# Mamba2 scan and SiLU block on one core: four PSUM banks shared by the scan and a correction sum, and another step plan

## The chip, the core and the metric

The kernel runs on one NeuronCore of a Trainium2 chip. The core has TensorE (PE, matmuls, with its weight loads shown as PEld), VectorE (DVE), ScalarE (ACT), GpSimd (POOL) and SyncE (SP, which here issues nearly all DMAs). Matmuls write to PSUM, which this program divides into eight banks of 128 x 512 fp32; everything else lives in SBUF. Each engine takes its instructions in the order in which the program issues them and waits on semaphores for the others. The metric is the time of one execution on the device in microseconds. Before the change it is 402.47 us, the median of two runs (402.38 and 402.56).

## The reference

Inputs: x (4 batches, 8 heads, 768 positions, 32), decays a (4, 8, 768), B and C (4, 8, 768, 16), w_in (256 x 2048) and w_out (2048 x 256), all fp32. The first half is a state-space scan in chunks; the second is a dense layer, SiLU, and a dense layer over 3072 tokens of 256 values:

```python
for c in range(nc):
    cum = np.cumsum(la, axis=-1)                       # la = log(clip(a, 1e-6, 1))
    L = np.exp(cum[:, :, :, None] - cum[:, :, None, :]) * causal
    M = np.einsum('bhin,bhjn->bhij', Cc, Bc) * L
    y[:, :, sl] = M @ xc + (Cc @ state) * np.exp(cum)[..., None]
    state = exp(sum la) * state + sum_j decay_from_j * B_j x_j
x = y.transpose(0, 2, 1, 3).reshape(3072, 256)
h = x @ w_in
g = h / (1 + np.exp(-h))
return g @ w_out
```

(The state's lines are shortened.)

## The kernel before, in words

**Tiling.** The 3072 tokens are twelve units of 256 (three a batch), in six pairs of 512 tokens, P = 0 to 5. A unit is four chunks of 64 positions: 2 halves k of 128 partitions, each with 2 chunks c. For each unit the scan does, with the letters that the step plan uses:

- T, P: transposes B and C (`f_T`, VectorE, with the scaled copies ce on ScalarE), and makes running products of the decays (`f_P`, VectorE).
- 0, 1, 2: clips the decays (`f_E0`) and makes the matrix E of all decay products with two VectorE scans (`f_E1`).
- B, C: scales B by the last column of E (BT, GpSimd) and C by the running products (cw; GpSimd except in units 1 and 2).
- G: C B' for each head (`f_G`, small matmuls, L407). M: multiplies E by it in place (`f_M`, VectorE, L413).
- D: B'x of each chunk (`f_D0`, L392). S: carries the state over the chunks (VectorE, L427), s: splits it into two masked copies (ScalarE, L434).
- Y: the output, from the state (L450) and from M (L460), and its copy to SBUF (`f_X`, xf, L471).
- h, l, d: splits xf into xh, xl and xd for the dense layers (ScalarE, GpSimd, VectorE).

**The dense layers.** Pair 0 uses plain fp32 matmuls (`f_s1`, `f_s2`), with tiles m0 to m7 of the second layer. From pair 1 on every product is made of three fp32r matmuls: a value v is split into a high part h and a low part l, and d = h - 4096 l; the product is h h' + l l' plus a correction by d d'. A step s of 80 handles one of 16 slices f of 128 hidden columns of a pair (f = s mod 16). Its first layer takes 6 matmuls: two d d' (`s1_d`, L527), a scaling of their result in PSUM by ScalarE (L529), and four on top (`s1_h`, L535). Then ScalarE makes g by SiLU (L543) and gh (L545), GpSimd gl (L549), VectorE gd (L553). The second layer runs three steps later (`s2`, LAG = 3) with 6 matmuls: two d d' (L564) and four of h and l (L567, L568), each kind summed in banks of its own over 16 steps. At a pair's end `f_out` copies both out, `f_sub` subtracts, `f_store` transposes and stores.

**The order of work.** It is written out by hand: nothing is scheduled by a planner. A list for pair 0 (`steps` and the texts with m) puts scan work for units 2 and 3 between the matmuls. Then `step(s)` issues the first layer of slice s, the second of slice s - 3, gd of s - 1 and the scan work of the next pair's units a (from f = 0) and b (from f = 6) by PLAN:

```python
PLAN = ("TP", "012BC", "GM", "gm", "DSs", "Y", "y", "hld")
```

So in step f = 7 unit a's h, l, d stand ahead of unit b's 0, 1, 2, B, C. The letters g, m and y are the second halves of G, M and Y. Loads of a unit two further on are issued behind y.

**Buffers.** PSUM: one pair of banks named gy, used in turn by both halves of G, by D and by both halves of Y; two single banks for the first layer (hp); four for the second layer's sums (two for h and l, two for d d'). A tile with one buffer can be written anew only once everything that reads it has finished. In SBUF, E, BT, ce, cw and sm have one buffer each, the loads of a unit two, x three; seven large buffers (quad) hold raw weights and later xh, xl and xd.

The weights come as raw words, are turned into fp32 (w_size on ScalarE, w_bits on VectorE and GpSimd) and split into wh, wl, wd: 0 to 9 in the prologue, 10 to 15 in pair 1.

Of the kernel before, what the change touches and what calls it, by code (L numbers as in the profile page):

```python
# [31 lines left out]
def kernel(  # L32
# [36 lines left out]
    loads = ctx.enter_context(tc.tile_pool(name="loads", bufs=2))  # L69
    quad = ctx.enter_context(tc.tile_pool(name="quad", bufs=7))  # L70
# [5 lines left out]
    ps_a = ctx.enter_context(tc.tile_pool(name="ps_a", bufs=4, space=bass.MemoryType.PSUM))  # L76
# [3 lines left out]
    NB = 66  # L80
# [8 lines left out]
    def bank2():  # L89
        return ps_s.tile([128, 2, 512], FP32, name="gy")  # L90
# [24 lines left out]
    def load_n(u, i, q):  # L115
        b, t0 = at(u)
        if i == 0:
            t = bn[u] = loads.tile([128, 2, H, N], FP32, name="bn")
        else:
            t = tbc[u] = loads.tile([128, 2, 2, 8, N], FP32, name="tbc")[:, 0]  # L120
        for k in range(2):
            q.dma_start(out=t[:, k], in_=(B, C)[i][b, :, t0 + 128 * k:t0 + 128 * k + 128].rearrange("h p n -> p h n"))

    def load_t(u, i, q):
        b, t0 = at(u)
        if u not in tbc:
            tbc[u] = loads.tile([128, 2, 2, 8, N], FP32, name="tbc")
        for g in range(4):
            q.dma_start(out=tbc[u][32 * g:32 * g + 32, i],
                        in_=(B, C)[i][b, 2 * g:2 * g + 2, t0:t0 + UT].rearrange("e (t r) n -> t e r n", r=8))  # L130

    def load_x(u, q):
        b, t0 = at(u)
        xt[u] = loads.tile([128, 2, H, D], FP32, name="xt", bufs=3)
        for k in range(2):
            q.dma_start(out=xt[u][:, k], in_=x[b, :, t0 + 128 * k:t0 + 128 * k + 128].rearrange("h p d -> p h d"))
# [17 lines left out]
    RAW = 7  # L154
# [59 lines left out]
    pz = const.tile([128, 8, Q + 1], FP32, name="pz")  # L214
    one = const.tile([128, 8, Q + 1], FP32, name="one")
    pfx01 = const.tile([128, 8, Q + 1], FP32, name="pfx01")
# [68 lines left out]
    E, M, BT, BH, CT, CE, CW, PFX, ST, SM, GY, XF, BX = ({} for _ in range(13))  # L285

    def f_P01():
        nc.vector.tensor_scalar(out=pz[:, :, 1:], in0=pa01.rearrange("p (c t) -> p c t", c=8), scalar1=1.0,
                                scalar2=1e-6, op0=ALU.min, op1=ALU.max)
        nc.vector.tensor_tensor_scan(out=pfx01.rearrange("p c t -> p (c t)"), data0=pz.rearrange("p c t -> p (c t)"),  # L290
                                     data1=one.rearrange("p c t -> p (c t)"), initial=0.0,
                                     op0=ALU.mult, op1=ALU.add)
        for u in range(2):
            PFX[u] = pfx01[:, 4 * u:4 * u + 4]

    def f_P0(u):
        nc.vector.tensor_scalar(out=pz[:, 0:4, 1:], in0=pa.pop(u).rearrange("p (c t) -> p c t", t=Q),
                                scalar1=1.0, scalar2=1e-6, op0=ALU.min, op1=ALU.max)

    def f_P1(u):  # L300
        PFX[u] = sc2.tile([128, 4, Q + 1], FP32, name="pfx")
        nc.vector.tensor_tensor_scan(out=PFX[u].rearrange("p c t -> p (c t)"),
                                     data0=pz[:, 0:4].rearrange("p c t -> p (c t)"),
                                     data1=one[:, 0:4].rearrange("p c t -> p (c t)"), initial=0.0,
# [73 lines left out]
    def f_D0(u, early=False):  # L378
# [3 lines left out]
        n = 3 if last else 4  # L382
        if early:
            d = [acc("bx")[:, 0:128] for c in range(2)]
        else:
            t = bank2()
            d = [t[:, c, 0:128] for c in range(2)]
        d = [o.rearrange("p (k x) -> p k x", k=2) for o in d]
        for t in range(n):
# [8 lines left out]
    def f_G(u, i):  # L398

        bh, ce = BH[u], CE[u]  # L400
        GY[u] = bank2()
        for c in range(2):
            for k in range(2):
                ts = slice(128 * k + 64 * c, 128 * k + 64 * c + 64)
                for q in range(2):
                    g = 2 * i + q
                    nc.tensor.matmul(out=GY[u][64 * c:64 * c + 64, q, 128 * k:128 * k + 128],  # L407
# [3 lines left out]
    def f_M(u, i):  # L411
        m = E[u].rearrange("p k (i q e) t -> p k i q (e t)", q=2, e=2)[:, :, i]
        nc.vector.tensor_tensor(out=m, in0=GY.pop(u)[:, :, 0:UT].rearrange("p q (k x) -> p k q x", k=2), in1=m, op=ALU.mult)  # L413
# [23 lines left out]
    def f_Y(u, e):  # L437


        sp, cw, m, xc = SM[u], CW[u], E[u], xt[u]  # L440
        y = GY[u] = bank2()
        opened = set()
        for k in range(2):
            for w in range(2):
                t = 2 * k + (w ^ e)
                if t == 0 and u % UPB == 0:
                    continue
                for q in range(2):
                    g = 2 * w + q
                    nc.tensor.matmul(out=y[64 * q:64 * q + 64, w, 64 * k:64 * k + 64],  # L450
                                     lhsT=sp[32 * g:32 * g + 32, t], rhs=cw[32 * g:32 * g + 32, Q * t:Q * t + Q],
                                     start=(w, q) not in opened, stop=False,
                                     tile_position=(32 * g, 64 * q), skip_group_check=True)
                    opened.add((w, q))
        for k in range(2):
            for w in range(2):
                c = w ^ e
                for q in range(4):
                    h = 4 * w + q
                    nc.tensor.matmul(out=y[32 * q:32 * q + 32, w, 64 * k:64 * k + 64],  # L460
                                     lhsT=xc[64 * c:64 * c + 64, k, h], rhs=m[64 * c:64 * c + 64, k, h],
                                     start=False, stop=True, tile_position=(64 * c, 32 * q), skip_group_check=True)

    def f_X(u, e):

        if e == 0:
            XF[u] = block("xf")
        y = GY.pop(u)
        o = two(XF[u]).rearrange("p w (k c t) -> p w k c t", k=2, c=2)
        for w in range(2):  # L470
            nc.scalar.activation(o[:, w, :, w ^ e], y[:, w, 0:128].rearrange("p (k t) -> p k t", k=2), AF.Copy)  # L471
# [83 lines left out]

    def s2(s):
        P, f = 1 + s // NF, s % NF
        if f == 0:
            OA[P] = [[acc("oa") for m in range(2)] for i in range(2)]
        n, r = 8 + f // 2, f % 2  # L560
        gh, gl, gd = GH.pop(s), GL.pop(s), GD.pop(s)
        for m in range(2):
            ms = slice(128 * m, 128 * m + 128)
            nc.tensor.matmul(out=OA[P][1][m], lhsT=two(WD[n])[:, r, ms], rhs=gd, start=(f == 0), stop=(f == NF - 1))  # L564
        for m in range(2):
            ms = slice(128 * m, 128 * m + 128)
            nc.tensor.matmul(out=OA[P][0][m], lhsT=two(WH[n])[:, r, ms], rhs=gh, start=(f == 0), stop=False)  # L567
            nc.tensor.matmul(out=OA[P][0][m], lhsT=two(WL[n])[:, r, ms], rhs=gl, start=False, stop=(f == NF - 1))  # L568
# [8 lines left out]
    def f_out(P):  # L577

        for m in range(2):
            t, o = block("od"), block("o")  # L580
            nc.scalar.activation(t, OA[P][1][m], AF.Copy)  # L581
            nc.vector.tensor_scalar(out=o, in0=OA[P][0][m], scalar1=UP, scalar2=None, op0=ALU.mult)
            OUT.append((P, m, o, t))
# [27 lines left out]
    f_G(0, 0)  # L611
# [4 lines left out]
    f_D0(0, True)  # L616
    f_P01()
# [4 lines left out]
    f_G(0, 1)  # L622
# [6 lines left out]
    f_Y(0, 0)  # L629
    f_X(0, 0)  # L630
    f_Y(0, 1)
    f_Ek(1, 0)
    f_Ab(1, 1)
    f_X(0, 1)
# [12 lines left out]
    f_G(1, 0)  # L647
    f_D0(1, True)
    f_M(1, 0)
    f_G(1, 1)  # L650
    f_S(1)
    f_SM(1)
    w_size(3)
    f_M(1, 1)
# [3 lines left out]
    f_Y(1, 0)  # L658
    f_X(1, 0)
    f_Y(1, 1)  # L660
    f_X(1, 1)
# [4 lines left out]
    def stage(u, what):  # L666
        for c in what:
# [20 lines left out]
            elif c in "Gg":  # L688
                f_G(u, "Gg".index(c))
            elif c in "Mm":  # L690
                f_M(u, "Mm".index(c))
            elif c == "D":
                f_D0(u)
            elif c == "S":
# [3 lines left out]
            elif c in "Yy":  # L698
                f_Y(u, "Yy".index(c))
                f_X(u, "Yy".index(c))  # L700
# [7 lines left out]
    def todo(text):  # L708

        for step in text.split():  # L710
            if ":" in step:
# [7 lines left out]
             (1, 4, "2:P0"), (0, 5, "2:12BC s9 3:L"), (1, 5, "2:GM b9 s10"), (0, 6, "2:gm"), (1, 6, "2:DSs b10 s11"),  # L719
             (0, 7, "2:Y b11 s12 3:T"), (1, 7, "2:y b12 s13 3:P0 h0"))  # L720
# [3 lines left out]
    for text in ("m0 3:12BC 2:h h1 l0 d0 2:l b13 s14", "m1 3:GM 2:d 4:L h2 l1 d1 b14 s15", "m2 3:gm h3 l2 d2 b15",  # L724
                 "m3 3:DSs h4 l3 d3", "m4 3:Y h5 l4 d4 h6", "m5 3:y l5 d5 5:L h7", "m6 3:hld l6 d6 h8", "m7 l7 d7 l8 d8 h9 o0 o1 l9 d9"):
# [5 lines left out]
    PLAN = ("TP", "012BC", "GM", "gm", "DSs", "Y", "y", "hld")  # L731
    WAITING = []

    def step(s):

        last = NF * (NP - 1)
        t = s - LAG
        ends = t >= 0 and t % NF == NF - 1
        if s < last:
            if s == 0:  # L740
                s1_d(0)
            if ends:
                s2(t)
            s1_h(s)
            if (s + 1) % NF:
                s1_d(s + 1)
            if ends:
                f_out(1 + t // NF)
            s1_g(s)
            s1_gl(s)  # L750
        if t >= 0 and (s >= last or not ends):
            s2(t)
        if s >= 1 and s - 1 < last:
            s1_gd(s - 1)
        if s >= last and ends:
            f_out(1 + t // NF)
            f_sub(nc.vector)
            f_store()
# [57 lines left out]
```

## Time and profile before

| | |
|---|---|
| median of the runs | 402.47 us |
| execution that was profiled | 407.98 us (span of the trace 406.2) |
| TensorE busy | 361.5 us (89%) |
| VectorE, ScalarE, GpSimd busy | 236.2, 214.1, 195.2 us |
| DMA | 26.37 MB, mean 65 GB/s |
| first fp32r step (s = 0) starts | 107.6 us |
| pair P = 1, then 2, 3, 4 | 61.6, then 58.7, 60.3, 58.8 us |
| last pair, without scan work, to the end | 59.2 us |
| SyncE's longest waits | for the output transposes, 214.1 us |

Times in the profile count from the first instruction. A row of a timeline or a chain gives start, duration, engine, line, operation and tiles (out<-in), then how often it is merged; in brackets stands how long the engine was idle before it and what ended that wait. Matmuls are pipelined, so a matmul's own duration (0.39) is longer than the distance to the next one (0.23); costs are read from starts. A busy share over the whole span mixes the prologue, the pairs with a scan and the last pair, so stretches are looked at one by one.

### The profile page before, as it was taken

The page shows a single profiled execution, that of the slowest core. Times are in us where ns is not written, and L with a number is a line of the kernel's source. Part 1 is how long each engine was busy: PE and PEld are TensorE (multiplying, and loading weights), DVE is VectorE, ACT ScalarE, POOL GpSimd, SP SyncE. Part 2 cuts the span into 40 slices and gives each one's busy share as a digit, 9 for nine tenths or more (in the row PEclk, how much of TensorE's full clock was granted, in tenths as well). Part 3 has the DMA queues.
Part 4 walks back from the last instruction along what each step waited for, and adds up shares of the span by engine and source line. Part 5 has one row for each costly group of instructions (what it writes and reads, how often), then busy time and mean ns, then how long its engine had stood idle before and what let it go on. Part 6 is the DMA issues. An engine that isn't in the chain of part 4 may idle for free.

```text
span 406.2 us, 7961 instructions
## 1 busy us (share of the span) xinstructions
PE 361.5 (89%) x3146; PEld 270.4 (67%) x3146; DVE 236.2 (58%) x345; ACT 214.1 (53%) x427; POOL 195.2 (48%) x168
## 2 busy tenths in 40 slices
PE   7798969989878969999979999799999799999990
PEld 3467757867656747767757767577767577768880
DVE  7377827995866574675661786541786542532223
ACT  2335726704466726665636656536656546475640
POOL 3134302476776465556353565334565445465440
PEclk9578969999999969999989999969999989999997
DMA  7887866340233150003670004750003000002003
GB/s 166 204 244 123 316 145 126 65 85 2 46 72 67 41 90 2 1 2 53 130 129 3 0 2 81 132 102 2 0 2 53 0 2 2 0 10 44 0 2 52
DMA packets 112621, 26.37 MB, mean 65 GB/s; under 512 B 102216, under 2 KB 108360, under 8 KB 112584
## 3 DMA queue, kind: packets, MB, share of 16 engines
q1 hardware_dynamic: 110504, 25.73, 30.3%
q8 instruction: 25, 0.41, 0.4%
q10 hardware_dynamic: 2080, 0.13, 0.3%
q14 instruction: 12, 0.10, 0.1%
HBM read 22.70 MB, written 3.15 MB: 64 GB/s over the span
## 4 chain that ended last, share of the span: by engine, by line
PE 50%; ACT 4%; POOL 4%; DVE 3%; issue 3%; DVEq 0%; POOLq 0%
PE hp L535 16%; PE hp L527 8%; PE oa L564 8%; PE oa L567 7%; PE oa L568 7%; POOL o L587 2%; ACT hp L529 2%; PE gy L450 1%; PE gy L407 1%; PE gy L460 1%; ACT od L581 1%; ACT g L543 1%; POOL gl L549 1%; DVE ot L596 1%; DVE E L413 1%
## 5 line engine op out<-in xcount | busy, mean ns | idle before, releaser
L549 POOL TENSOR_TENSOR gl<-g,gh 128x512 fp32r<-128x512 f32 x80 | 107.5, 1346 | 106.1 <-ACT gh L545 96.9
L553 DVE SCALAR_TENSOR_TENSOR gd<-gl,gh 128x512 fp32r<-128x512 f32 x80 | 76.0, 957 | 81.8 <-POOL gl L549 77.6
L529 ACT ACTIVATE hp<-hp 128x512 f32<-128x512 f32 x80 | 46.5, 581 | 88.4 <-PE hp L527 88.1
L535 PE MATMUL hp<-xh,wh 128*128 128x512 f32 x160 | 70.0, 437 | 6.7 <-ACT hp L529 6.4
L535 PE MATMUL hp<-xl,wl 128*128 128x512 f32 x160 | 64.8, 405 | 0.0
L567 PE MATMUL oa<-gh,wh 128*128 128x512 f32 x160 | 63.8, 399 | 0.0
L568 PE MATMUL oa<-gl,wl 128*128 128x512 f32 x160 | 63.7, 398 | 0.0
L527 PE MATMUL hp<-xd,wd 128*128 128x512 f32 x160 | 52.6, 410 | 1.2 <-ACT g L543 1.2
L545 ACT ACTIVATE gh<-g 128x512 fp32r<-128x512 f32 x80 | 50.5, 632 | 3.9
L564 PE MATMUL oa<-gd,wd 128*128 128x512 f32 x160 | 51.5, 404 | 0.0
L543 ACT ACTIVATE g<-hp 128x512 f32<-128x512 f32 x80 | 47.5, 594 | 3.0 <-PE hp L535 3.0
L535 PEld LDWEIGHTS hp<-xh,wh 128*128 128x128 f32 x160 | 30.6, 191 | 21.1 <-ACT hp L529 11.5
L191 POOL TENSOR_TENSOR w<-wu,wv 128x512 uint32<-128x512 uint32 (+1 forms) x20 | 21.5, 1082 | 43.2 <-DVE wv L186 41.8
L500 PE MATMUL hp<-xf,w 128*128 128x256 f32 x128 | 36.3, 443 | 4.7 <-DVE cw L375 3.7
L527 PEld LDWEIGHTS hp<-xd,wd 128*128 128x128 f32 x160 | 30.9, 195 | 10.2 <-ACT g L543 2.9
L564 PEld LDWEIGHTS oa<-gd,wd 128*128 128x128 f32 x160 | 31.2, 195 | 7.6
L314 DVE TENSOR_TENSOR_SCAN E<-ab,diag 128x512 f32<-128x512 f32 x24 | 32.5, 1390 | 6.3 <-PE gy L460 5.5
L500 PEld LDWEIGHTS hp<-xf,w 128*128 128x128 f32 x128 | 27.9, 224 | 11.9 <-issue 6.2
L567 PEld LDWEIGHTS oa<-gh,wh 128*128 128x128 f32 x160 | 31.0, 194 | 7.2
L568 PEld LDWEIGHTS oa<-gl,wl 128*128 128x128 f32 x160 | 30.8, 192 | 7.4
L535 PEld LDWEIGHTS hp<-xl,wl 128*128 128x128 f32 x160 | 31.0, 194 | 5.0
L407 PE MATMUL gy<-ce,bh 32*64 32x128 f32 x384 | 17.6, 297 | 15.7 <-DVE E L413 15.7
(84 smaller groups left out, 428.5 us busy)
## 6 DMA issues: line engine op xcount, KB each, us to landing
ab<-in_a_dram SPq DMA_DIRECT2D x40, 128.0 KB
raw<-in_moe_w_in_dram SPq DMA_DIRECT2D x8, 512.0 KB
raw<-in_moe_w_out_dram SPq DMA_DIRECT2D x8, 512.0 KB
xt<-in_x_dram SPq DMA_DIRECT2D x24, 128.0 KB
out_dram<-ot SPq DMA_DIRECT2D x48, 64.0 KB
bn<-in_B_dram SPq DMA_DIRECT2D x22, 64.0 KB
tbc<-in_C_dram SPq DMA_DIRECT2D x40, 32.0 KB
pa<-in_a_dram SPq DMA_DIRECT2D x10, 128.0 KB
```

Source lines behind the costliest of these rows:

```text
L314: nc.vector.tensor_tensor_scan(out=E[u].rearrange("p k h t -> p (k h t)")[:, Q * g0:Q * (g0 + n)], data0=t.rearrange("p g t -> p (g t)"), ...
L500: nc.tensor.matmul(out=hp[:, i], lhsT=two(w32[j])[:, kc, 128 * i:128 * i + 128], rhs=two(XF[u])[:, kc], start=(kc == 0), stop=(kc == KC - 1))
L527: nc.tensor.matmul(out=HP[s], lhsT=two(WD[f // 2])[:, kc, 128 * (f % 2):128 * (f % 2) + 128], rhs=XD[P][:, kc], start=(kc == 0), stop=Fals ...
L529: nc.scalar.activation(HP[s], HP[s], AF.Copy, scale=-1.0 / UP)
L535: nc.tensor.matmul(out=HP[s], lhsT=two(w[f // 2])[:, kc, 128 * (f % 2):128 * (f % 2) + 128], rhs=x_[P][:, kc], start=False, stop=(kc == KC ...
L543: nc.scalar.activation(G[s], HP.pop(s), AF.Silu, scale=UP)
L545: nc.scalar.activation(GH[s], G[s], AF.Copy, scale=DOWN)
L549: nc.gpsimd.tensor_tensor(out=GL[s], in0=G.pop(s), in1=GH[s].bitcast(FP32), op=ALU.subtract)
L553: nc.vector.scalar_tensor_tensor(out=GD[s], in0=GL[s].bitcast(FP32), scalar=-4096.0, in1=GH[s].bitcast(FP32), op0=ALU.mult, op1=ALU.add)
L564: nc.tensor.matmul(out=OA[P][1][m], lhsT=two(WD[n])[:, r, ms], rhs=gd, start=(f == 0), stop=(f == NF - 1))
L567: nc.tensor.matmul(out=OA[P][0][m], lhsT=two(WH[n])[:, r, ms], rhs=gh, start=(f == 0), stop=False)
L568: nc.tensor.matmul(out=OA[P][0][m], lhsT=two(WL[n])[:, r, ms], rhs=gl, start=False, stop=(f == NF - 1))
```

## The change

The second layer's sum of d d' gives up its own two banks and shares four banks with the scan (`bank4`). Those four serve, in turn, G and D of a unit together, its Y, and, twice a pair, a stretch of d d' sums. The scan's matmuls of a unit thus come in two bursts instead of five (G with D, Y whole). G's order of heads changes too: consecutive matmuls go to four different row groups. The d d' matmuls of a pair are put off and issued in clumps when the banks are free (`PENDING`, `s2_d`): a first segment at f = 5 to 7, a second from f = 11 to f = 2 of the next pair; after each, VectorE takes the sum to SBUF (`f_sum2`, copy and then add).

The step plan is new: h, l, d lie in steps of their own, and the weight splits 6, 7 and 9 to 15 lie in pair 1 (PARTS). The last two m pieces of pair 0 go into steps 0 and 1. `s1_d` of the next slice is issued in the same place in all steps. To make room in SBUF for 74 instead of 66 small blocks, the loads of a unit have one buffer, x two, quad six.

```diff
-    loads = ctx.enter_context(tc.tile_pool(name="loads", bufs=2))
-    quad = ctx.enter_context(tc.tile_pool(name="quad", bufs=7))
+    loads = ctx.enter_context(tc.tile_pool(name="loads", bufs=1))
+    quad = ctx.enter_context(tc.tile_pool(name="quad", bufs=6))
...
-    ps_a = ctx.enter_context(tc.tile_pool(name="ps_a", bufs=4, space=bass.MemoryType.PSUM))
+    ps_a = ctx.enter_context(tc.tile_pool(name="ps_a", bufs=2, space=bass.MemoryType.PSUM))
...
-    NB = 66
+    NB = 74
...
-    def bank2():
-        return ps_s.tile([128, 2, 512], FP32, name="gy")
+    def bank4(name="gy"):
+        return ps_s.tile([128, 4, 512], FP32, name=name, tag="gy")
...
-        xt[u] = loads.tile([128, 2, H, D], FP32, name="xt", bufs=3)
+        xt[u] = loads.tile([128, 2, H, D], FP32, name="xt", bufs=2)
...
-    RAW = 7
+    RAW = 6
...
+    def f_G(u):
+        bh, ce, dp = BH.pop(u), CE.pop(u), new_dp(u)
+        for k in range(2):
+            for c in range(2):
                 ts = slice(128 * k + 64 * c, 128 * k + 64 * c + 64)
...
+                for g in range(4):
+                    nc.tensor.matmul(out=dp[64 * c:64 * c + 64, g, 128 * k:128 * k + 128],
                                      lhsT=bh[32 * g:32 * g + 32, ts], rhs=ce[32 * g:32 * g + 32, :, ts],
                                      start=True, stop=True, tile_position=(32 * g, 64 * c), skip_group_check=True)
...
+    def f_sum2(P):
+
+        b2 = B2.pop(P)
+        if P not in SUM2:
+            SUM2[P] = [block("sum2") for m in range(2)]
+            for m in range(2):
+                nc.vector.tensor_copy(out=SUM2[P][m], in_=b2[:, m])
+        else:
+            for m in range(2):
+                nc.vector.tensor_tensor(out=SUM2[P][m], in0=b2[:, m], in1=SUM2[P][m], op=ALU.add)
...
+        f_sum2(P)
         for m in range(2):
-            t, o = block("od"), block("o")
-            nc.scalar.activation(t, OA[P][1][m], AF.Copy)
-            nc.vector.tensor_scalar(out=o, in0=OA[P][0][m], scalar1=UP, scalar2=None, op0=ALU.mult)
-            OUT.append((P, m, o, t))
+            o = block("o")
+            nc.scalar.activation(o, OA[P][m], AF.Copy, scale=UP)
+            OUT.append((P, m, o, SUM2[P][m]))
...
-    for text in ("m0 3:12BC 2:h h1 l0 d0 2:l b13 s14", "m1 3:GM 2:d 4:L h2 l1 d1 b14 s15", "m2 3:gm h3 l2 d2 b15",
-                 "m3 3:DSs h4 l3 d3", "m4 3:Y h5 l4 d4 h6", "m5 3:y l5 d5 5:L h7", "m6 3:hld l6 d6 h8", "m7 l7 d7 l8 d8 h9 o0 o1 l9 d9"):
+    for text in ("m0 3:12CB 2:h h1 l0 d0 2:l b13 s14", "m1 3:D 2:d 4:L h2 l1 d1 b14 s15", "m2 3:SsM h3 l2 d2 b15",
+                 "m3 3:Y h4 l3 d3", "m4 3:h h5 l4 d4 h8 3:l", "m5 3:d l5 d5 5:L l8 d8"):
         todo(text)
...
-    PLAN = ("TP", "012BC", "GM", "gm", "DSs", "Y", "y", "hld")
-    WAITING = []
+
+    PLAN = {0: ("aTP0",), 1: ("a12CB",), 2: ("aD",), 3: ("aSsM", "bL"), 4: ("aY",), 5: ("ah", "bTP0"), 6: ("al", "b12CB"),
+            7: ("ad",), 8: ("bD",), 9: ("bSsM", "aL"), 10: ("bY",), 11: ("bh",), 12: ("bl",), 13: ("bd",)}
+    PENDING = []
+
+    PARTS = {0: 9, 2: 10, 4: 11, 5: 6, 6: 12, 8: 7, 9: 13, 11: 14, 13: 15}
...
+        if ends and scans:
+            end()
         if s < last:
...
+        if PENDING and not (scans and (f < 5 or 8 <= f < 11)):
+            s2_d(PENDING)
+            PENDING.clear()
+        if scans and f == 7:
+            f_sum2(P)
```

In the new plan D stands for `f_G` and `f_D0` together, M for both halves, Y for the whole output and its copy, L for the loads of a unit. `scans` is true while a next pair remains to be scanned, and `ends` in the step in which a pair's last slice reaches the second layer (f = 2 of the next pair); there `end()` issues the clump of d d' and the last h and l matmuls first of all.

## The prediction

> **What bounds the kernel now.** I read the page first: shares of busy time and the slices.
>
> ```profile
> PE 361.5 (89%) x3146; PEld 270.4 (67%) x3146; DVE 236.2 (58%) x345; ACT 214.1 (53%) x427; POOL 195.2 (48%) x168
> PE   7798969989878969999979999799999799999990
> ...
> PEclk9578969999999969999989999969999989999997
> DMA  7887866340233150003670004750003000002003
> ```
>
> TensorE is nearly always busy, DMA is not after the first quarter, and the clock row has a dip once a pair (slices 15, 21, 27, 33). The second view, busy time by stretch, gives the pairs P = 2, 3, 4 and then the last pair with the tail:
>
> ```profile
> 71.20:107.60 36.40, 32.72 (x297) 26.64 (x282) 29.32 (x39) 14.56 (x32) 22.84 (x18) 1.00 0.22 42
> 107.60:169.20 61.60, 52.60 (x486) 38.32 (x486) 37.95 (x52) 36.14 (x72) 38.08 (x30) 0.94 0.29 52
> 169.20:227.90 58.70, 54.99 (x504) 41.02 (x504) 34.95 (x51) 34.04 (x68) 29.66 (x25) 0.97 0.30 55
> 227.90:288.20 60.30, 56.44 (x497) 41.89 (x497) 34.64 (x50) 34.06 (x68) 29.33 (x25) 0.94 0.30 54
> 288.20:347.00 58.80, 55.01 (x504) 40.99 (x504) 34.64 (x50) 34.08 (x68) 29.57 (x25) 0.97 0.06 10
> 347.00:406.20 59.20, 48.87 (x208) 38.76 (x208) 19.91 (x28) 29.10 (x51) 24.54 (x19) 0.96 0.11 19
> ```
>
> After the length of each stretch come PE, PEld, DVE, ACT, POOL, then the granted clock. A pair takes 58.7 to 60.3 us. The chain, in the last pair where no scan runs, shows what a step costs when only TensorE counts:
>
> ```profile
> 365.42 0.93 PE hp L535 x4
> ...
> 368.20 0.93 PE hp L535 x4
> ```
>
> The pitch is 2.78 us for twelve matmuls, 0.232 each: 16 steps are 44.5. The rest of a scanning pair, 14 to 16 us, is small matmuls and waits. The timeline of TensorE shows both:
>
> ```profile
> 199.12 0.39 PE L568 MATMUL oa<-gl,wl 128*128 128x512 f32 x1
> 199.44 0.68 PE L407 MATMUL gy<-ce,bh 32*64 32x128 f32 x16
> 200.05 0.50 PE L535 MATMUL hp<-xh,wh 128*128 128x512 f32 x1
> 200.38 0.40 PE L535 MATMUL hp<-xl,wl 128*128 128x512 f32 x1
> ...
> 205.61 0.68 PE L407 MATMUL gy<-ce,bh 32*64 32x128 f32 x16 [2.51 <-DVE E L413]
> 206.22 0.68 PE L535 MATMUL hp<-xh,wh 128*128 128x512 f32 x1
> 206.70 0.63 PE L535 MATMUL hp<-xl,wl 128*128 128x512 f32 x1
> ```
>
> From 199.12 to 200.38 is 1.26 us; two ordinary spacings (0.46) would have been there anyway, so half a G costs 0.80, of which 0.61 is the burst and 0.19 entry and exit. The same subtraction gives 0.58 for D (185.27 to 186.31) and 0.96 for half a Y (192.59 to 194.01). A unit is 2 x 0.80 + 0.58 + 2 x 0.96 = 4.1 us, two are 8.2. So 52.7 of a pair is work, and 6 to 7.6 us is lost. Most of that is at 205.61: the second half of G waits 2.51 us for VectorE, and then the matmuls run at a spacing of 0.43 instead of 0.23 (step 10 takes 4.90 us where 3.36 are due). Together 4.2 us a pair, more in the two pairs whose clock stays low for longer. VectorE's timeline tells why:
>
> ```profile
> 199.85 0.69 DVE L490 SCALAR_TENSOR_TENSOR xd<-xl,xh 128x512 fp32r<-128x512 f32 x1 [3.62 <-POOL xl L486]
> ...
> 201.41 2.34 DVE L314 TENSOR_TENSOR_SCAN E<-ab,diag 128x512 f32<-128x512 f32 x2
> 203.66 0.67 DVE L553 SCALAR_TENSOR_TENSOR gd<-gl,gh 128x512 fp32r<-128x512 f32 x1
> 204.86 0.69 DVE L413 TENSOR_TENSOR E<-gy,E 128x512 f32<-128x512 f32 x1 [0.53 <-POOL BT L347]
> ```
>
> In step 7 the xd of unit a stands ahead of unit b's scans, and waits 3.62 us for an xl issued to GpSimd in the same step. The scans come late by that, then the first M, and the second G needs the banks that this M reads.
>
> [...] the idle 2.51 us is followed by 3.4 us at a spacing near 0.43, while an idle 1.58 us (at 88.97) leaves the clock at 1.00. [...]
>
> **The change, part by part.**
>
> *Bursts.* G and D become one burst, Y one. Three entries and exits a unit go: at least 3 x 0.19 = 0.57. G now alternates over eight tile positions instead of four; its 32 matmuls lie between 0.61 (all parallel) and 1.22 (no gain); I take 0.75. With D (0.39) and one entry: 1.33. Y: 1.92 less 0.19 to 0.5, since the change between the two kinds inside it also goes once; I take 1.5. Sum 2.8 a unit (2.6 to 3.5), 1.3 less than now.
>
> *Step plan.* xh, xl, xd of unit a move to steps 5, 6, 7, its scans' neighbours to 6: the wait of xd is gone, M doesn't stand between two halves of G. That takes away the 4.2 us of every pair, if nothing replaces it. s1_d of the next pair is issued in its ordinary place in step 15 and not at the end: step 15 falls from 3.62 to 2.78, 0.8 a pair.
>
> *d d' sum.* The same 32 matmuls a pair, only clumped; cost 0 on TensorE. The sum now leaves PSUM in two pieces: two PSUM reads more on VectorE a pair, near 0.68 each (as M and the o copy, 0.683 and 0.668), in place of nothing. VectorE has the time on average (35 of 59 us), but the first piece's two reads stand between its scans and G. Step 8: the clump and steps 5 to 7 give TensorE 3.7 + 2.8 + 2.8, and G is due 2.3 later, 11.6 us after step 5 begins. VectorE starts a gd at 2.0, then come transposes, prefix scan and clip (3.1), a gd, two scans (2 x 1.43) and the reads (1.36): with gd at 0.67 to 0.96 it ends at 10.7 to 11.3. Cost 0 to 0.5, hidden by the matmuls of s1 and s2. Step 2: here only two steps lie between (2.33 each, as d d' is put off), and G is due 3.73 us after step 2 begins, 8.4 after step 0. VectorE: gd of step 15 ends at 2.5 (5.1 after step 15's start, as at 229.42), transposes, P and clip to 5.6, gd 6.5, scans 9.4, two reads 10.8. G waits 2.3 us; with blocked or free GpSimd 1.3 to 3. Behind it on TensorE stand all of step 3's matmuls. This is in P = 2, 3, 4 alone. A wait of this size halves the clock in about every second case (1.58 didn't, 2.5 did), 2 us each: 1.0 in the mean. 3.3 a boundary.
>
> *Steps with ten matmuls* (0, 1, 3, 4, 8 to 10) have 2.33 us for ScalarE's three operations, 1.75 us, and the hp copy must return within the step. Extra SM or ce (0.7 to 0.9) there delays it: I allow 1.0 a pair, and 0.3 for the rest.
>
> *A pair*: 44.5 + 5.6 + 3.3 + 1.0 + 0.3 = 54.7. Three pairs: 164 instead of 178.
>
> *71.2 to 169.2.* Two of the eight m pieces move from the prologue into steps 0 and 1, where TensorE now waits for ScalarE. Work: m 8 x 3.65 = 29.2; units 3, 4, 5 at 2.8 = 8.4; s1 98 matmuls = 22.8; s2 78 = 18.2; together 78.6. With 5 for waits (weight splits now lie in this pair: 9 of them, three more than now, 0.9 us of VectorE each; xd of unit 3 just ahead of s1_d) 83.6 instead of 98.0, where the waits of 3.39 and 1.38 us and the low clock lie.
>
> *Start to 71.2.* Units 1 and 2 save 1.3 each. In unit 0 the second G half waits 2.49 us for M at 11.61, which goes, and P is half as long. The 3.7 us before 54.03 stay: same order of scans and cw. One raw weight fewer in flight delays loads; loads were 78% busy here. 66.5 instead of 71.2.
>
> *Loads with one buffer.* A unit's loads take about 10 us to issue (190.69 to 201.3). Unit b's may start when a's P, scans and BT are through, 5 to 11 us after step 0, and are needed from step 5, 16 us after it. I cost them at nothing: scans of the unit before hide them, with 2 us to spare.
>
> *Last pair and tail*: 58.2 instead of 59.2; the end has the same two reads and two subtractions.
>
> Sum: 66.5 + 83.6 + 164.1 + 58.2 = 372.4, against 406.2 of this trace. The profiled execution took 407.98 us, 5.5 more than the median of 402.47; part of that is the longer low clock of two dips (6.8 instead of 3.4 us), which falls away in the changed kernel too. I put 1.8 for the ends of the program and -1.5 for calmer dips: 373 us.
>
> **Rivals.**
> 1. The bank waits take most of it: VectorE hands over late in step 2 and step 8, the clock drops each time, and G doesn't speed up. 3.5 pairs x (2.3 + 1) more, plus 8 x 0.7 for slower bursts: 373 + 11.5 + 5.6 = 390. For it: one buffer serves six uses a pair, gd's are often blocked. Against: step 8 has its own slack.
> 2. Slower than before: single-buffered loads or the chain S, SM, M, Y, X, d d', sum don't fit the steps, and each of the 8 units 4 to 11 waits 3 us, with the clock low behind it for another 1.5: 373 + 8 x 4.5 = 409. For it: 10 us to issue a unit's loads. Against: SyncE is idle for most of a pair.
> 3. Better: step 2's wait is about 1 us and never halves the clock, and the start speeds up because unit 0 keeps the clock high: 373 - 3 x 2.3 - 4 = 362.
>
> **How the numbers follow.** Forecast (365 to 383) 0.62; rival 1 (383 to 397) 0.19; rival 2 0.07; rival 3 (under 365) 0.12. A change within 2% is 394.4 to 410.5: the upper edge of rival 1 and half of rival 2, 0.08. Range 361 to 391: it leaves out rival 2, the top of rival 1 and the lowest of rival 3.
>
> **What would show it.** Right: no idle of 2.5 us before a G in step 9; xd without a wait for xl; one G burst of x32 with 0.6 to 0.9 us to the next start; step 15 at 2.8; a pair at 53 to 56; TensorE waiting 1 to 3 us at G of step 2 for VectorE's sum. Wrong: waits at Y for M or SM, at the d d' clump for X, VectorE's transposes waiting for a DMA, more clock dips than one a pair, or a start that is longer than 71 us for want of weights.

## The result, and the profile after

The changed kernel takes 389.06 us (median of 388.22 and 389.90), against 402.47 before: 0.967 of the time, with a 95% interval of 0.958 to 0.976. The forecast was 373. The gain is 13.4 us where 29.5 were expected: less than half. The time lies inside the stated range, and next to rival 1's 390. Ratios and intervals use fast executions alone, and the profiled execution of the kernel before was a slow one (407.98 us), so that lengths read from its trace are in sum some 5.5 us too long.

The page's shares and its clock row, for the kernel after:

```profile
PE 337.8 (87%) x3146; PEld 263.3 (68%) x3146; DVE 254.7 (66%) x355; ACT 211.9 (55%) x403; POOL 209.0 (54%) x168
...
PEclk9999899989998799969999989999989999999997
```

TensorE is busy for 24 us less, VectorE for 18 us more, and there is still a dip of the granted clock in every scanning pair (a stretch at a granted clock of 0.50, here for 3.4 to 6.8 us). Busy time by stretch (length, then PE, PEld, DVE, ACT, POOL, clock), where the first line is pair 1, the next three are the pairs 2, 3, 4 and the last is the pair without a scan and the tail:

```profile
88.70:151.40 62.70, 56.13 (x518) 44.24 (x519) 44.54 (x54) 37.71 (x72) 41.83 (x31) 0.95 0.28 51
151.40:212.30 60.90, 53.37 (x506) 41.21 (x505) 42.22 (x55) 33.69 (x65) 34.64 (x25) 0.94 0.28 53
212.30:270.60 58.30, 51.81 (x497) 40.58 (x496) 39.70 (x51) 33.59 (x65) 33.13 (x24) 0.97 0.29 56
270.60:328.80 58.20, 51.92 (x505) 40.68 (x504) 39.78 (x51) 33.64 (x65) 33.14 (x24) 0.97 0.18 33
328.80:386.50 57.70, 48.58 (x209) 38.75 (x208) 18.94 (x27) 29.83 (x52) 25.50 (x19) 0.96 0.11 19
```

The pairs 2 to 4 took 177.8 us before and take 177.4 now: nearly all of the gain between the two traces (406.2 to 386.5) lies ahead of pair 2 (17.8 us) and behind pair 4 (1.5 us). In the pairs 2 to 4 TensorE's busy time fell by 1.6, 4.6 and 3.1 us, and 3.8, 2.6 and 2.5 us of idle time came in. Its timeline in steps 2 and 3 of pair 4 shows where:

```profile
278.49 0.63 PE L513 MATMUL hp<-xd,wd 128*128 128x512 f32 x2
282.63 0.70 PE L397 MATMUL gy<-ce,bh 32*64 32x128 f32 x32 [3.51 <-DVE sum L579]
...
283.82 0.79 PE L521 MATMUL hp<-xh,wh 128*128 128x512 f32 x1
284.42 0.63 PE L521 MATMUL hp<-xl,wl 128*128 128x512 f32 x1
284.84 0.63 PE L521 MATMUL hp<-xh,wh 128*128 128x512 f32 x1
```

The old wait of 2.51 us between the halves of G is gone. In its place the whole G waits 3.51 us for VectorE's `f_sum2`, and the matmuls behind it run at a spacing of 0.43 again. Steps 8 and 10 of the same pair, in TensorE's timeline:

```profile
304.23 0.70 PE L397 MATMUL gy<-ce,bh 32*64 32x128 f32 x32 [0.94 <-DVE sum L576]
305.84 0.43 PE L385 MATMUL gy<-xt,BT 64*32 64x64 f32 x24 [0.91 <-POOL BT L341]
...
312.05 0.69 PE L437 MATMUL gy<-cw,sm 32*64 32x64 f32 x32 [0.92 <-ACT hp L515]
```

Three more waits of nearly 1 us each: G for the sum, D for BT, Y for M (its last input to be ready, VectorE's M, ends at 311.9; the row names an earlier release). The steps of pair 4, measured from first h matmul to first h matmul, add up to what is lost. In steps 1 and 2 the clump of six d d' matmuls lies in front of step 2's first h matmul.

| step | 0 | 1 | 2 | 3 | 4 | 5 | 6, 7 | 8 | 9 | 10 | 11 | 12 to 15 |
|---|---|---|---|---|---|---|---|---|---|---|---|---|
| us | 2.32 | 4.62 | 6.26 | 3.78 | 3.83 | 3.81 | 2.78 | 5.40 | 2.44 | 4.82 | 4.26 | 2.78 |
| without a wait | 2.32 | 4.62 | 2.5 | 2.33 | 3.83 | 3.72 | 2.78 | 3.4 | 2.33 | 3.83 | 4.2 | 2.78 |

(The second row counts matmuls at 0.232 us, G with D at 1.08 and Y at 1.5, both as steps without waits have them.) Steps 2 and 3 lose about 5.2 us, step 8 2.0, step 10 1.0.

VectorE's timeline and then GpSimd's for the same stretch tell why the sum is late:

```profile
277.52 3.87 DVE L308 TENSOR_TENSOR_SCAN E<-ab,diag 128x512 f32<-128x512 f32 x2
281.32 1.26 DVE L579 TENSOR_TENSOR sum<-b,sum 128x512 f32<-128x512 f32 x2
```

```profile
277.12 1.64 POOL L535 TENSOR_TENSOR gl<-g,gh 128x512 fp32r<-128x512 f32 x1 [1.71 <-ACT gh L531]
278.72 1.60 POOL L369 TENSOR_TENSOR cw<-ct,pfx 128x256 f32<-128x256 f32 x1
281.47 0.64 POOL L341 TENSOR_TENSOR BT<-bn,E 128x256 f32<-128x256 f32 x1 [1.16 <-DVE E L308]
```

The two reads of the sum are short (1.26 us together), and the clump that they read was ready long before. They stand behind the two scans, which took 3.87 us where I had put 2.86, while gl and cw ran on GpSimd. BT, which D needs, is later still by construction: it can't start before the second scan has ended.

### The profile page after: what moved, and what is told of

It reads as the page before. It is cut to its first block, busy times and chain, and to the rows that moved or that the text cites. A ratio compares the mean times of both kernels' runs of the same rounds, so it can differ in the third digit from the quotient of the medians.

```text
span 386.5 us, 7896 instructions
## 1 busy us (share of the span) xinstructions
PE 337.8 (87%) x3146; PEld 263.3 (68%) x3146; DVE 254.7 (66%) x355; ACT 211.9 (55%) x403; POOL 209.0 (54%) x168
## 4 chain that ended last, share of the span: by engine, by line
PE 48%; DVE 30%; issue 9%; ACT 5%; POOL 4%; DMA 2%; DVEq 0%; SPq 0%; POOLq 0%; ACTq 0%
PE hp L521 12%; DVE E L308 8%; PE hp L513 5%; PE b L567 5%; PE oa L554 5%; PE oa L553 5%; DVE gd L539 4%; PE hp L486 4%; PE oa L499 4%; POOL gl L535 3%; PE gy L446 2%; DVE st L417 2%; PE gy L437 2%; DMA raw<-in_moe_w_out_dram 2%; DVE E L403 2%
## 5 line engine op out<-in xcount | busy, mean ns | idle before, releaser
L535 POOL TENSOR_TENSOR gl<-g,gh 128x512 fp32r<-128x512 f32 x80 | 113.0, 1416 | 106.1 <-ACT gh L531 91.6
L521 PE MATMUL hp<-xh,wh 128*128 128x512 f32 x160 | 67.6, 423 | 1.8 <-ACT hp L515 1.8
L554 PE MATMUL oa<-gl,wl 128*128 128x512 f32 x160 | 64.1, 400 | 0.0
L513 PE MATMUL hp<-xd,wd 128*128 128x512 f32 x160 | 52.2, 408 | 0.3 <-ACT g L529 0.3
L567 PE MATMUL b<-gd,wd 128*128 128x512 f32 x160 | 45.4, 392 | 0.0
L308 DVE TENSOR_TENSOR_SCAN E<-ab,diag 128x512 f32<-128x512 f32 x24 | 41.0, 1742 | 0.7 <-PE ab L315 0.5
L194 POOL TENSOR_TENSOR w<-wu,wv 128x512 uint32<-128x512 uint32 (+1 forms) x20 | 22.5, 1131 | 31.1 <-DVE wv L189 31.1
L567 PEld LDWEIGHTS b<-gd,wd 128*128 128x128 f32 x160 | 30.0, 188 | 7.0 <-DVE gd L539 0.3
L486 PE MATMUL hp<-xf,w 128*128 128x256 f32 x128 | 31.5, 401 | 3.6 <-DVE cw L369 1.8
L210 POOL TENSOR_TENSOR wd<-wh,wl 128x512 fp32r<-128x512 f32 x16 | 23.8, 1496 | 13.3 <-DVE wl L205 13.3
L486 PEld LDWEIGHTS hp<-xf,w 128*128 128x128 f32 x128 | 24.7, 199 | 9.1 <-POOL w L194 2.6
```

Of the source, the lines that this page charges most:

```text
L308: nc.vector.tensor_tensor_scan(out=E[u].rearrange("p k h t -> p (k h t)")[:, Q * g0:Q * (g0 + n)], data0=t.rearrange("p g t -> p (g t)"), ...
L486: nc.tensor.matmul(out=hp[:, i], lhsT=two(w32[j])[:, kc, 128 * i:128 * i + 128], rhs=two(XF[u])[:, kc], start=(kc == 0), stop=(kc == KC - 1))
L513: nc.tensor.matmul(out=HP[s], lhsT=two(WD[f // 2])[:, kc, 128 * (f % 2):128 * (f % 2) + 128], rhs=XD[P][:, kc], start=(kc == 0), stop=Fals ...
L521: nc.tensor.matmul(out=HP[s], lhsT=two(w[f // 2])[:, kc, 128 * (f % 2):128 * (f % 2) + 128], rhs=x_[P][:, kc], start=False, stop=(kc == KC ...
L535: nc.gpsimd.tensor_tensor(out=GL[s], in0=G.pop(s), in1=GH[s].bitcast(FP32), op=ALU.subtract)
L554: nc.tensor.matmul(out=OA[P][m], lhsT=two(WL[n])[:, r, ms], rhs=gl, start=False, stop=(f == NF - 1))
```

## The experiments

All times are compared with the kernel before on the same chip (its medians there were 399.9 to 400.9 us). The changed kernel itself was run only twice, and its interval (0.958 to 0.976) is wide, so small differences from it are read from single steps in the traces and not from totals.

**Are the reads of the sum the cost?** The sums are made but not read.

```diff
-        b2 = B2.pop(P)
-        if P not in SUM2:
-            SUM2[P] = [block("sum2") for m in range(2)]
...
-                nc.vector.tensor_tensor(out=SUM2[P][m], in0=b2[:, m], in1=SUM2[P][m], op=ALU.add)
+        B2.pop(P)
+        SUM2[P] = [diag.rearrange("p h t -> p (h t)") for m in range(2)]
```

> The d d' sums are still made but never read: VectorE's reads of them are left out, and a constant is subtracted in their place (the output lacks this correction). Theory 1 (VectorE's scans are late in steps 1 and 6, and the reads only add to that): D then waits for BT where G waited for the sum; a scanning pair P = 2 to 4 falls from 58.2 by about 3 (1.2 at step 2, 0.9 at step 8, 1.1 at Y in step 10), the whole to about 379 us. Rival (the hand-over of the four banks to VectorE is the cost): the whole 3.5 and 0.9 and the low clock behind it go, 6 to 7 a pair, the whole to about 368 us.

It took 387.85 us, 0.970 of the time before (0.964 to 0.975; the changed kernel 0.967). The pairs 2 to 4 take 60.6, 56.4 and 58.0 us. TensorE in step 2 of pair 3:

```profile
220.01 0.69 PE L397 MATMUL gy<-ce,bh 32*64 32x128 f32 x32
223.49 0.43 PE L385 MATMUL gy<-xt,BT 64*32 64x64 f32 x24 [2.78 <-POOL BT L341]
```

G no longer waits, and D, one burst on, waits 2.78 us for BT. So the hand-over of the banks is not by itself the cause: the scans are late, and taking the sum away uncovers the next thing that waits for them. The pairs became shorter by 0.3, 1.9 and 0.2 us, even less than the 3 us a pair that I expected of my own theory.

**Scans a step earlier (unit a).**

```diff
-    PLAN = {0: ("aTP0",), 1: ("a12CB",), 2: ("aD",), ...
+    PLAN = {15: ("nTP0",), 0: ("a12CB",), 2: ("aD",), ...
```

(n is unit a of the pair after; for unit 4 the work goes into the text of m5.)

> Unit a's T, P, 0 move from step 0 to step 15 of the pair before and its scans, C and B from step 1 to step 0; all else as in the changed kernel. Theory 1 (scans late): the wait at G in step 2 (3.5 us) and the low clock behind it (1.5) go in three pairs, about 374 us. Rival (the hand-over itself takes it, or the wait moves to D, to Y or to step 8): 385 us or more.

0.953 (0.948 to 0.958; this interval just touches the changed kernel's), a median of 381.07 us where 374 was expected. TensorE in step 2 of pair 3:

```profile
220.03 0.63 PE L513 MATMUL hp<-xd,wd 128*128 128x512 f32 x2
221.70 0.70 PE L397 MATMUL gy<-ce,bh 32*64 32x128 f32 x32 [1.04 <-DVE sum L579]
```

The wait falls from 3.5 to 1.04 us, with the sum still read, and the clock doesn't drop behind it (spacing 0.23). VectorE's scans in the same pair are as long as ever, only earlier:

```profile
215.98 3.89 DVE L308 TENSOR_TENSOR_SCAN E<-ab,diag 128x512 f32<-128x512 f32 x2
```

The pairs take 56.6, 55.0 and 54.7 us: 4.3, 3.3 and 3.5 less. Step 8 keeps its waits, 0.94 and 0.89 us, and in pairs 2 and 3 the clock now dips behind them (in pair 3 D takes 0.56 us instead of 0.43). Theory 1 holds in its place: the three pairs give 11 of the 15 us expected. In the whole it is some 6 us (0.967 to 0.953), since this execution came to pair 2 3.9 us later (155.3 instead of 151.4; its early dip of the clock lasted 10.2 us instead of 3.4).

**Output subtraction out of step 5.**

```diff
-        if t > 2 and t % NF == 2:
+        if t > 6 and t % NF == 6:
             f_sub()
-        if t > 4 and t % NF == 4:
+        if t > 8 and t % NF == 8:
             f_store()
```

> Only GpSimd's subtraction of the outputs moves from step 5 to step 9, and the store from step 7 to step 11. Theory 1: this 3 us of GpSimd blocks gd and unit b's scans on VectorE; without it the waits of G and D in step 8 (0.9 each) and of Y in step 10 (1.1) go in three pairs: about 381 us, step 2 unchanged. Rival (gl, xl and cw block the scans anyway): 387 us or more.

0.963 (0.957 to 0.969), 385.80 us where 381 was expected, and not to be told from the changed kernel. But step 8 itself answers: it falls from 5.4 us to between 3.4 and 3.5 in all three pairs. In the changed kernel VectorE's scans of unit b, and GpSimd beside them, stood thus in pair 4:

```profile
298.53 4.47 DVE L308 TENSOR_TENSOR_SCAN E<-ab,diag 128x512 f32<-128x512 f32 x2
302.92 1.26 DVE L576 COPY sum<-b 128x512 f32<-128x512 f32 x2
```

```profile
296.76 2.98 POOL L598 TENSOR_TENSOR o<-o,sum 128x512 f32<-128x512 f32 x2
299.71 2.21 POOL L535 TENSOR_TENSOR gl<-g,gh 128x512 fp32r<-128x512 f32 x1
301.88 2.21 POOL L472 TENSOR_TENSOR xl<-xf,xh 128x512 fp32r<-128x512 f32 x1
```

and with the subtraction moved VectorE has, in pair 3:

```profile
242.63 2.33 DVE L308 TENSOR_TENSOR_SCAN E<-ab,diag 128x512 f32<-128x512 f32 x2
246.20 1.29 DVE L576 COPY sum<-b 128x512 f32<-128x512 f32 x2 [1.24 <-PE b L567]
```

The two scans take 2.33 us instead of 4.47, and now VectorE waits for TensorE's clump and not the other way round. The three pairs take 172.9 us instead of 177.4, but this execution came to pair 2 at 155.5 instead of 151.4, again with more low clock early on, and in pair 3 the dip behind step 2 lasted 6.8 us instead of 3.4: both hide it in the total. Y's wait in step 10, which I had put down to the same cause, stayed.

**BT ahead of cw.**

```diff
-    ... 1: ("a12CB",), ... 6: ("al", "b12CB"),
+    ... 1: ("a12BC",), ... 6: ("al", "b12BC"),
```

> In steps 1 and 6 BT comes before cw on GpSimd, so that GpSimd reads nothing while the second scan runs. Theory (GpSimd's reads hold up VectorE's scans): the second scan of step 1 falls from 1.63 us to its free 1.17, and the wait at G of step 2 from 3.5 to about 3.0. Rival (the scans got longer for another reason): durations stay at 2.3 and 1.6 us. The whole: 386 to 389 us in either case.

VectorE in step 1 of pair 4:

```profile
285.71 3.43 DVE L308 TENSOR_TENSOR_SCAN E<-ab,diag 128x512 f32<-128x512 f32 x2
```

3.43 instead of 3.87: the second scan takes 1.19 instead of 1.63, and G's wait falls by just that, from 3.51 to 3.07. D no longer waits for BT in step 8. But the single run took 399.54 us, with pairs of 63.6, 61.6 and 61.4 us. GpSimd now stands idle until the scans are over and gl comes later; S and M stand behind two gd that take 3.47 us (2.38 in the changed kernel), and Y in step 10 waits 2.98 us instead of 0.92, with a dip of the clock each time (spacing 0.43 in pair 4). My figure for the whole was wrong by over 10 us.

**The old order of G in the new burst.**

```diff
-        for k in range(2):
-            for c in range(2):
+        for i in range(4):
+            for k in range(2):
+                c = i % 2
...
-                for g in range(4):
+                for g in range(2 * (i // 2), 2 * (i // 2) + 2):
```

> G of the changed kernel issued in the order of the kernel before (two row groups at a time), still one burst of 32. If the new order lets eight tiles run side by side, a G burst goes from 0.70 back to about 1.3 us; the rival (the order does nothing) leaves 0.70. The whole rises by at most 0.6 for each of 12 units, less where D waits for BT anyway: 389 to 394 us.

390.72 us in one run. TensorE in step 8 of pair 3:

```profile
248.39 0.74 PE L398 MATMUL gy<-ce,bh 32*64 32x128 f32 x32 [0.94 <-DVE sum L577]
```

0.74 us instead of 0.70: the rival holds. 32 matmuls in one burst take hardly longer than 16 did alone (0.68), in either order. So the forecast's size of the burst was near (0.63 us from its start to D's in pair 4, where I took 0.75) and its reason, the new order, wrong; why the second half comes nearly free is open. That matmuls on different tiles run side by side was my estimate; the run doesn't show it.

**The kernel before with one edit.** Unit a's h, l, d are spread over three steps, and nothing else.

```diff
-                if 0 <= f - base < len(PLAN):
+                plan = PLANS[i]
+                if 0 <= f - base < len(plan):
...
-    WAITING = []
+    PLANS = (PLAN[:-1] + ("h", "l", "d"), PLAN)
```

> The kernel before with one edit: unit a's h, l, d are spread over steps 7, 8 and 9, so that xd no longer stands ahead of unit b's scans. The prediction's reading (xd's wait for xl makes the second G late): 4.2 us go in each of four pairs, about 386 us, as fast as the whole change. Rival (the second G waits for M behind the scans in any case): 397 us or more.

0.968 (0.962 to 0.973), as fast as the whole change. Its pairs 2 to 4 by stretch:

```profile
160.10:215.80 55.70, 53.48 (x505) 39.94 (x505) 37.80 (x51) 33.93 (x68) 31.04 (x25) 1.00 0.32 58
215.80:271.50 55.70, 53.43 (x496) 39.90 (x496) 37.50 (x50) 33.93 (x68) 30.88 (x25) 1.00 0.32 58
271.50:327.20 55.70, 53.46 (x504) 39.95 (x504) 37.52 (x50) 33.99 (x68) 30.89 (x25) 1.00 0.06 11
```

The clock stays at 1.00, and a pair takes 55.7 us: shorter than the changed kernel's, with five bursts a unit. The reading of the wait at 205.61 was right, its size too large: steps 9 and 10 fall from 6.17 and 4.90 us to 3.59 and 4.4, which is 3.1 of the forecast's 4.2 us. The wait of 2.51 us and the low clock are gone, but in step 10 D now waits nearly 1 us. The trace names no releaser; in pair 2 VectorE's second M, which stands behind gd and xd and reads the banks that D needs, ends at 198.52, and D starts right behind:

```profile
198.62 0.46 PE L392 MATMUL gy<-xt,BT 64*32 64x64 f32 x32 [0.99 <-issue]
```

(In pair 3, where the old trace's clock was low for 6.8 us instead of 3.4, 4.5 us go.) In the pairs the change thus took this gain, added that of the bursts, and paid both back in the new waits.

**Both moves together**: scans a step earlier and the subtraction later.

> Both moves at once: unit a's T, P, 0, 1, 2, C, B a step earlier, and the output subtraction and store four steps later. If the two waits are separate, steps 2 and 8 both run at their cost and a pair takes 53 to 54 us: about 377 us. If one only covers the other, no better than 381.

0.938 (0.932 to 0.945), 376.85 us. Pairs of 54.4, 52.9 and 52.8 us, no dip in any of them, steps 2 and 8 at 3.7 and 3.4 (in step 2 a wait of 1.1 us for the sum is left). The two waits are separate, and with neither of them long the granted clock is 1.00 in all three pairs.

**S, s, M in the step of G and D.**

```diff
-    ... 2: ("aD",), 3: ("aSsM", "bL"), ... 8: ("bD",), 9: ("bSsM", "aL"), ...
+    ... 2: ("aDSsM",), 3: ("bL",), ... 8: ("bDSsM",), 9: ("aL",), ...
```

> As the run with both moves, and S, s, M issued in the step of G and D (2 and 8) instead of the next one, so that they stand ahead of one gd fewer on VectorE. The wait of Y in step 10 (1.1 us) goes, in four pairs: about 373 us. Rival (SM blocks ScalarE's hp copies, or M wasn't what Y waited for): 377 or more.

0.952 (0.946 to 0.958), slower than without. ScalarE, then TensorE, in step 9 of pair 3:

```profile
249.73 0.64 ACT L424 ACTIVATE sm<-st,par 128x96 f32<-128x96 f32 x2 [3.91 <-DVE st L417]
250.27 0.57 ACT L515 ACTIVATE hp<-hp 128x512 f32<-128x512 f32 x1
```

```profile
250.90 0.50 PE L521 MATMUL hp<-xh,wh 128*128 128x512 f32 x1 [2.43 <-ACT hp L515]
```

Y's wait went (step 10 falls to 3.9), but sm now waits for S at the head of ScalarE's queue, with the hp copy that TensorE needs next behind it: 2.43 us. The rival holds.

**Weight splits of pair 1 out of steps 5 to 8**, on top of both moves.

```diff
-    PARTS = {0: 9, 2: 10, 4: 11, 5: 6, 6: 12, 8: 7, 9: 13, 11: 14, 13: 15}
+    PARTS = {0: 9, 1: 10, 2: 11, 3: 12, 4: 6, 9: 7, 10: 13, 11: 14, 13: 15}
```

> As the run with both moves, and the weight splits of pair 1 taken out of steps 5 to 8: 9, 10, 11, 12, 6 in steps 0 to 4, then 7, 13, 14, 15 in 9, 10, 11, 13. Theory (what stands ahead of the scans and the sum on VectorE decides when G, D and Y can go, here the splits too): pair 1 falls from 64 us to about 58, the whole to about 371. Rival (pair 1 is long because of the two m pieces and the clock): pair 1 stays above 62, the whole at 376.

0.927 (0.920 to 0.935), 372.75 us; the interval overlaps that of both moves alone. Pair 1 falls from 64.1 to 61.2 us, less than expected; G in step 8 still waits 1.65 us for the sum. The theory's direction holds, its size for this pair doesn't.

**gd of step 8 behind S and M**, on top of that.

```diff
-        if 1 <= s <= last:
+        if 1 <= s <= last and not (scans and f == 9):
             s1_gd(s - 1)
...
+        if scans and f == 9:
+            s1_gd(s - 1)
```

> As the run with moved splits, and in step 9 the gd of step 8 comes after S and M of unit b on VectorE instead of before them. Theory (S and M stand behind a gd that waits for a gl): the wait of Y in step 10 (1.1 us) goes in four pairs, about 4 us less than the run with moved splits. Rival (Y waits for SM on ScalarE or for cw): no difference.

0.923 (0.918 to 0.928), 369.61 us, the fastest of all; its interval overlaps that of the run before it. Step 10 falls by 0.6 in each of the pairs 2 to 4 (4.96 to 4.36 in pair 3), not by 1.1. Its stretches, pairs 2, 3, 4:

```profile
151.00:204.80 53.80, 50.50 (x506) 39.43 (x505) 39.42 (x56) 33.71 (x65) 34.38 (x25) 1.00 0.31 60
204.80:257.00 52.20, 50.43 (x497) 39.33 (x496) 38.73 (x52) 33.57 (x65) 32.66 (x24) 1.00 0.33 62
257.00:309.20 52.20, 50.58 (x506) 39.50 (x505) 37.81 (x51) 33.73 (x65) 32.70 (x24) 1.00 0.20 36
```

50.4 of 52.2 us are TensorE's work: the bursts' gain, spent in the changed kernel on waits, is now kept.

## Why the prediction was wrong, point by point

Between the traces I forecast 406.2 to 372.4 us, and the changed kernel's is 386.5. Of these 14.1 us, 13.3 lie in the pairs 2 to 4 (164.1 forecast, 177.4 measured), -0.5 in the last pair, and 1.3 ahead of pair 2.

*What was right.* The wait for xd in step 7, and that taking it away makes the pairs shorter (shown by the one edit of the kernel before); of its 4.2 us a pair 3.1 came in two of three pairs, and a wait of D took the place of the rest. G with D at 1.1 and Y at 1.5 us a unit: 2.6, the lower of my bounds, where I took 2.8. Step 15 at 2.78. No wait for a load was found in the pairs; in the prologue ScalarE waits once for a weight (4.8 us), and behind that TensorE stands idle until 40.6, for 3.7 us. That one raw weight fewer in flight is the reason was not tested apart. And the place of the new wait: G of step 2, for VectorE's sum, with VectorE's queue right to half a microsecond up to the scans (gd of step 15 due to end 2.5 us after step 0 begins, in the trace 2.6; the scans due to begin at 6.5, in the trace 6.9).

*The step that failed: "two scans (2 x 1.43)", and with it what I allowed for waits in a pair.* I took the mean of a scan in the old trace as its cost in the new place. This is the line of the kernel before, for pairs 2 to 4 (after the bar, busy us and the mean in ns):

```profile
L314 DVE TENSOR_TENSOR_SCAN E<-ab,diag 128x512 f32<-128x512 f32 x10 | 13.9, 1432 | 0.4
```

The mean is of short and long ones. The profile of this one group in the kernel before, after, and in the fastest version (min/median/max in ns):

```profile
L314 DVE TENSOR_TENSOR_SCAN E<-ab,diag x24: 1156/1220/2334, 5.5 to 321.6; 128x512 f32<-128x512 f32 x24
```

```profile
L308 DVE TENSOR_TENSOR_SCAN E<-ab,diag x24: 1191/1631/2318, 5.4 to 300.8; 128x512 f32<-128x512 f32 x24
```

```profile
L308 DVE TENSOR_TENSOR_SCAN E<-ab,diag x24: 1191/1222/2320, 5.4 to 281.5; 128x512 f32<-128x512 f32 x24
```

A scan takes 1.2 us alone and up to 2.3 beside a GpSimd operation. The plan decides which: in step 1 gl and cw fall on the scans, and in step 6 the 3 us subtraction, gl and xl, so two took 3.87 us in step 1 (2.86 forecast) and 4.47 in step 6. The runs show that it is what stands beside them: with the subtraction moved two take 2.33 us instead of 4.47, and with cw moved the second takes 1.19 instead of 1.63. The old trace has the same for gd, 0.67 to 0.70 us in the 45 cases without GpSimd beside it and 1.31 in the mean of the other 35. I had seen gd's spread there and priced the scans by an average all the same.

The terms of a pair, forecast and measured in pair 4: G's wait in step 2, 2.3 and 3.5; low clock behind it, 1.0 and about 1.5; step 8, 0 to 0.5 and 2.0; Y in step 10, nothing and 1.0; ScalarE in the ten-matmul steps and the rest, 1.3 and about 0.5; the bursts, 5.6 and 5.2. 54.7 became 58.2. In pair 2 the dip lasted 6.8 us instead of 3.4, step 1 took 5.84 us instead of 4.62, and the pair 60.9. Of the wait in step 2 the order of VectorE's queue alone gave the 2.3 us that I had forecast, and the longer scans 1.0 more; in step 8 the moved subtraction, with scans 2.1 us shorter, takes the whole difference away. Y's wait for M in step 10 I had named as a sign of being wrong, and had put no cost on it.

*D was costed behind G.* I let G wait for the sum and D follow. D waits for BT and BT for the last scan, so leaving out the sum uncovers a wait of 2.78 us. The chain behind a late scan has two ends, and I had followed one.

*Rival 1* forecast the time, 390, and two of its three reasons: late hand-over in steps 2 and 8, and clock dips. Its third, that G doesn't speed up, is wrong, and the 5.6 us that it put on it didn't come; it had put 11.5 us on the waits, and the pairs 2 to 4 alone lost 13.3. So its 390 is in part luck. I gave it 0.19 and the main case 0.62, having seen in the old trace that gd often took longer (0.67 at its shortest, 0.96 in the mean), and argued that step 8 had slack of its own. It had, without the subtraction: 3.44 us.

*Two errors cancelled ahead of pair 2*, so that the 1.3 us there is luck. The first m piece starts at 59.7 instead of the 66.5 forecast, and from there to pair 2 it takes 91.7 us instead of 83.6: pair 1 has G's wait of 3.06 in step 8 and Y's of 2.33 in step 10, behind the weight splits. Part of the fast start is no merit of the change: in the old trace the clock was low for 13.7 us early on, and the kernel before with the one edit, whose prologue is the same, had a dip of 3.4 there and reached step 0 at 100.7 us instead of 107.6. The profiled execution of the kernel before was 5.5 us longer than its median. I put 1.5 us for that; the trace of after is 0.8 below its own median, so that some 6 us of what the two traces differ by aren't in the medians.

*The clock.* From one idle time of 2.51 us with a dip behind it and one of 1.58 us without, the forecast took the length of a wait as what decides, and put a dip behind every second one. That was an estimate from two cases: without the reads of the sum, a wait of 2.78 us in pair 3 had no dip behind it. The last section has what the traces show.

*Left open*: what makes a dip last 6.8 us instead of 3.4; why 32 matmuls of G take hardly longer than 16; and what holds G in step 8 of pair 1 with the splits moved.

## What to carry to other kernels

When an instruction moves to another place on its engine, don't carry its mean duration along: look at its shortest and longest, ask what made the difference, and whether that will run beside it in the new place. When a wait is removed, look for the second consumer of the same late producer, since it will wait next; here leaving out the sum moved the wait from G to D and gained next to nothing, and in the kernel before the one edit uncovered a wait of 1 us at D. And before rebuilding buffers to remove a wait, try the smallest edit of the order of issue: spreading three operations over three steps gave as much as the whole change.

## What the runs showed of the hardware that was not expected

A VectorE scan of 128 x 512 took 1.16 to 1.23 us in the 25 cases of the traces of before and after in which GpSimd ran nothing beside it, and 1.19 to 2.33 us in the other 23. Such a delay costs TensorE twice where TensorE waits for it: in pair 4 of the changed kernel 3.5 us of waiting, of which 1.0 was the longer scans, and another 1.5 at half the matmul rate (spacing 0.43 instead of 0.23). 32 small matmuls in one burst took 0.70 us where 16 took 0.68.

Whether the clock dropped behind a wait did not go by the length of the wait alone. In the traces of before and after a dip lasted 3.41 or 6.83 us (once 13.65, from 11.8 us on in the kernel before; the last ran to the end), and the times at which the clock changed lay whole multiples of 3.41 us apart. Cut at these times into stretches of 3.41 us, each with the share that TensorE's matmul records fill (some records can be missing from a trace), the two traces show this: of the stretches at full clock, all 14 filled to less than 45% were followed by half clock, neither of the 2 between 45 and 55%, and 1 of the 189 above (filled to 67%). Without the reads of the sum, D's wait is 2.78 us in pair 3 and 2.79 in pair 4. In pair 3 it falls on two stretches (the first two lines, 2.07 and 1.97 us of TensorE), and there is no dip; in pair 4 it falls into one (0.62 us), and there is (length of the stretch, then PE, PEld, DVE, ACT, POOL, clock):

```profile
218.64:222.05 3.41, 2.07 (x39) 1.27 (x37) 3.41 (x2) 1.93 (x4) 2.64 (x2) 1.00 0.22 60
222.05:225.46 3.41, 1.97 (x31) 1.62 (x32) 1.64 (x4) 0.77 (x2) 2.24 (x2) 1.00 0.32 44
276.66:280.07 3.41, 0.62 (x55) 0.38 (x47) 2.67 (x3) 2.55 (x5) 2.25 (x3) 1.00 0.14 38
```

The two waits of 0.9 us in step 8 are the same case. In pair 4 of the changed kernel they lie in two stretches (2.84 and 2.14 us of TensorE) and the clock stays; with unit a's scans moved they share one in pairs 2 and 3 (1.73 and 1.58 us), and it drops.
